# An mLSTM cell and a squared-ReLU feed-forward on one core: gates in two steps, a bf16 mask, the first tiles in another order, and loads placed after y's store

## The chip, the cores and the metric

The kernel runs on one core of one Trainium2 chip. The metric is the device time in microseconds (us); the time before is the median of five runs.

## The reference

Two blocks are joined. The first is an mLSTM cell with batch B = 4, heads H = 8, sequence S = 768 and head size D = 40, all in float32. The second treats the result as 3072 tokens of 320 values.

```python
for t in range(S):
    m_new  = max(f_gate[t] + m, i_gate[t])
    f_stab = exp(f_gate[t] + m - m_new);  i_stab = exp(i_gate[t] - m_new);  m = m_new
    C = f_stab * C + i_stab * outer(v[t], k[t])          # D x D for each head
    n = f_stab * n + i_stab * k[t]
    y[t] = sigmoid(o_gate[t]) * (C @ q[t]) / max(abs(n @ q[t]), 1)
x = y, transposed to (B*S, H*D) = (3072, 320)
out = maximum(x @ w_in, 0)**2 @ w_out                    # w_in 320 x 2048, w_out 2048 x 320
```

## The kernel before

**Tiles.** The sequence is cut into chunks of 128 positions, six for each batch entry (NB = 6), which gives 24 tiles s = 0 to 23 (NT), each with all 8 heads. Two tiles form a group g = 0 to 11 (NG) of 256 tokens for the feed-forward.

**The cell in chunks.** With the gates summed up inside a chunk (A, and b = i - m - A), the decay between two positions of a chunk is exp(A + b). For a tile the kernel turns k and q (`transposes`), multiplies them (`scores`), makes the decays W (`weigh`), multiplies the two into P (`weighted`), and multiplies P by v, with a column of ones that yields the denominators (`attend`). The state C goes from tile to tile. `normalise` applies the denominator and the output gate and gives x; `turn_rows` turns x into xT, the operand of the feed-forward. From tile 6 and 7 on, turned operands come by DMA through scratch in DRAM: `store_num` and `load_num` carry the numerators, `store_rows` and `load_rows` carry x, and 32x32 block transposes on VectorE finish the turn (`normalise_turned`, `turn_squares`, `turn_kq`). `load_squares` reads k and q from a scratch that `pair_up` writes.

**The gates.** `do_gates` runs once, on 32 rows (batch and head) of 768 columns: a scan for m, some elementwise steps, and a scan for A that restarts at each chunk. `turn_gates` turns b and A. For tiles 0 and 1 A is spread over 128 partitions by TensorE (`spread_A`): a matmul of a 128x128 identity by the causal mask `later` (0 or -1e30), 512 columns wide, starts each half, and four matmuls with selector matrices add the heads' rows. From tile 2 on, A goes by DMA to DRAM (`a_rows`) and is read back broadcast (`load_A`), and GpSimd masks it (`mask`).

**Weights.** The weights come as two 32-bit words for each value. A `Rounding` object takes 26 pieces: `fetch` loads a piece (SyncE's queue, four buffers), `words` converts its parts on ScalarE, and `join` combines them on VectorE and GpSimd and fetches the next piece into the freed buffer.

**Order.** Nothing is planned at run time: the order of the program is the order on each engine, and semaphores guard the data. The program has three parts. The prefix is written out by hand and ends with the first feed-forward matmul; `idle(n)` puts n filler matmuls of 512 columns into TensorE's stream there. Then come eight steps u = 0 to 7 in which tiles 2 to 5 are mixed with the first feed-forward products. Then comes a list of parts (which, g, i) with counter n: which = 1 is a quarter of the first product of group g, which = 2 a step of the second. From n = 8 on, r = n % 8 gives the place in a batch of eight parts and b = 7 + 2 * (n // 8) its tile:

| r | part | around it, before the change |
|---|---|---|
| 0, 1 | second product, steps 0 and 1 of group g | r = 0: turn_squares(b-2), sums; after it normalise and store_rows of b-1; r = 1: load_rows(b-1) |
| 2 to 5 | first product of group g+2 | r = 3 and 5: score and attend_turned of the next tiles; r = 3: store_num, load_num of b |
| 5 | (as above) | ahead: normalise_turned(b), store_rows(b); after: store_num(b+1), load_rows(b), load_num(b+1), load(b+5), load_o |
| 6, 7 | second product, steps 2 and 3 of group g | r = 6: load_squares(b+3); r = 7: load_A(b+4) |

**The second product.** It is made from seven half products (`product`, 16 matmuls of 160 columns each; a matmul is two instructions in float32) with sums of operands (`sums`, `sums_of_weights`) on VectorE. The results are added into two y tiles out of a ring of three (`y_sb`). Step 2 issues the store of y1 (L779), step 3 that of y0 (L784), both on SyncE's queue, which also issues all loads. The first of the next group's adds into y0 reuses the buffer of the y1 stored just before.

Of the kernel before, what the change touches and what calls it, by code (L numbers as in the profile page):

```python
# [29 lines left out]
def kernel(  # L30
# [79 lines left out]
    later = gates.tile([P, P], F32)  # L110
# [5 lines left out]
    def make_consts():  # L116
# [6 lines left out]
        make_identity(nc, ident[:])  # L123

# [120 lines left out]
    def do_gates():  # L245
        nc.vector.tensor_tensor_scan(m_sb[:], f_sb[:], i_sb[:], -1e30, op0=ALU.add, op1=ALU.max)
        nc.vector.memset(f_sb[:, 0:1], 0.0)
        nc.vector.tensor_tensor(f_sb[:, 1:], f_sb[:, 1:], m_sb[:, : S - 1], op=ALU.add)
        nc.vector.tensor_tensor(f_sb[:, 1:], f_sb[:, 1:], m_sb[:, 1:], op=ALU.subtract)
        nc.vector.tensor_scalar_max(f_sb[:], f_sb[:], LOG_ZERO)  # L250
        nc.vector.tensor_tensor_scan(
            A_sb[:], keep[:].rearrange("p c t -> p (c t)"), f_sb[:], 0.0, op0=ALU.mult, op1=ALU.add,
        )
        nc.vector.tensor_tensor(i_sb[:], i_sb[:], m_sb[:], op=ALU.subtract)
        nc.vector.tensor_tensor(i_sb[:], i_sb[:], A_sb[:], op=ALU.subtract)

    def turn_gates():
        for src, dst in ((i_sb, b_T), (A_sb, eA_T)):
            tp = ps_o.tile([P, W], F32, name="tp", tag="o_ps")[:, : S // P * BH].rearrange("p (c r) -> p c r", r=BH)
            for c in range(NB):  # L260
                nc.tensor.transpose(tp[:, c, :], src[:, c * P : (c + 1) * P], ident[:BH, :BH])
            nc.scalar.activation(
                dst[:].rearrange("p b c h -> p c b h"), tp.rearrange("p c (b h) -> p c b h", b=B),
                AF.Copy if dst is b_T else AF.Exp,
            )
# [72 lines left out]
    def spread_A(s):  # L338

        b, c = divmod(s, NB)  # L340
        H2 = H // 2
        d = st.setdefault(s, {})
        d["A"] = []
        for i in range(2):
            A = ps_h.tile([P, H2, P], F32, name="A_ps", tag="h_ps")
            nc.tensor.matmul(
                A[:], lhsT=ident[:], rhs=later[:].unsqueeze(1).to_broadcast([P, H2, P]), start=True, stop=False,
            )
            for h in range(H2):
                nc.tensor.matmul(  # L350
                    A[:, h, :], lhsT=sel[:, i * H2 + h, :], rhs=A_sb[:, c * P : (c + 1) * P],
                    start=False, stop=(h == H2 - 1),
                )
            d["A"].append(A)
# [49 lines left out]
    def transposes(s, o=(False, False), apart=0):  # L404
        d = st[s]
        kqT(s)
        for i, n in enumerate(("kT", "qT")):
            if i > 0 and apart:
                idle(apart)
            tp = bank(o[i])  # L410
            for j in range(PR):
                nc.tensor.transpose(
                    tp[:, j, :], d["kq"][:, i, 2 * j : 2 * j + 2, :].rearrange("p h d -> p (h d)"), ident[:],
                )
            (nc.scalar.copy if i == 0 or s in (0, *range(2, 7)) else nc.vector.tensor_copy)(d[n], tp)
# [13 lines left out]
    def weighted(s, spare=False):  # L429
        d = st[s]  # L430
        d["P"] = []
        for i in range(2):
            t = ffn.tile([P, W], F32, name="r_sb", bufs=4) if spare else work.tile([P, W], F32, name="P_sb")
            t = t[:].rearrange("p (j t) -> p j t", j=PR)
            d["P"].append(t)
            heads = slice(i, H, 2) if s < KQ_SQ else slice(PR * i, PR * (i + 1))
            nc.vector.tensor_tensor(t, d["sc"][i], d["W"][:, heads, :], op=ALU.mult)  # L437
# [380 lines left out]
    fetch(2)  # L818
    make_consts()
    load_part(1, 0)  # L820
    load_part(1, 1)
    load_part(0, 2)
    fetch(1)
# [3 lines left out]
    fetch(1)  # L827
    idle(12)
    transposes(0, apart=4)
    idle(4)  # L830
    scores(0)
    idle(3)
    do_gates()
    rounding.words()
    nc.scalar.dma_start(A_d[:, :], A_sb[:])
    spread_A(0)
    rounding.words()
    turn_gates()
    rounding.join()
    weigh(0)  # L840
    transposes(1, (False, True))
    spread_A(1)
    scores(1, (True, True))
    weigh(1)
    first.close()
# [3 lines left out]
    weighted(0)  # L849
    weighted(1, spare=True)  # L850
# [7 lines left out]
    rounding.step()  # L858
    sum_of_h(0)
    normalise(0)  # L860
    mask(2)
    attend(1)
    sum_of_h(1)
    normalise(1)
    load(3)
    load_A(3)
    rounding.step()
    turn_rows(0)
    idle(4)
    transposes(2)  # L870
    idle(4)
# [128 lines left out]
    for n, (which, g, i) in enumerate(parts):  # L1000
# [39 lines left out]
        if r == 0 and g > 1:  # L1040
            do(turn_squares, b - 2)
            sums(g, ALL, (3,))
# [3 lines left out]
        elif r == 5:  # L1046
            do(normalise_turned, b)
            do(store_rows, b)
        elif r == 7 and g < NG - 1:
            sums(g + 1, ALL, (2,))  # L1050
# [91 lines left out]
        elif r == 5:  # L1142
            do(store_num, b + 1)
            do(load_rows, b)
            do(load_num, b + 1)
            do(load, b + 5)
            for t in range(b + 5, min(b + 7, NT)):
                load_o(t)
        elif r == 6:
# [3 lines left out]
        elif r == 7:  # L1153
            do(load_A, b + 4)
        if which == 2 and g == NG - 1 and i == 0:
            sums(g, ALL, (4,))
# [33 lines left out]
```

## Time and profile before

| quantity | value |
|---|---|
| median of the runs | 533.61 us (532.84 to 534.18, five runs) |
| profiled execution | 535.23 us, span 533.4 us, mean granted TensorE clock 0.989 |
| TensorE | busy 513.6 us (96%) |
| TensorE weight load | busy 451.8 us (85%) |
| VectorE | busy 331.7 us (62%) |
| ScalarE | busy 193.9 us (36%) |
| GpSimd | busy 90.6 us (17%) |
| DMA | 68.06 MB, mean 128 GB/s |
| first feed-forward matmul (L649) starts | 32.30 us |

The span runs from the first to the last instruction of one profiled execution; the rest of that execution's time lies around it. In the profile PE is TensorE, PEld its weight load, DVE is VectorE, ACT is ScalarE, POOL is GpSimd, and SP is SyncE; a q behind a name is that engine's queue or sequencer. L649 is line 649 of the kernel before. Rows of the timeline give start, duration, engine, line, operation, output <- input, the number of instructions merged, and in brackets the idle time before it with what ended it. A busy TensorE is not a TensorE at full use: filler counts as busy, and so does a matmul at half clock.

### The profile page before, as it was taken

To read this page: it belongs to the slowest core of one execution; us is meant where nothing else is said; L and a number is where in the kernel's file an instruction comes from. 1 tells how busy PE (TensorE), PEld (TensorE's weight loads), DVE (VectorE), ACT (ScalarE), POOL (GpSimd) and SP (SyncE) were. 2 spreads that over 40 slices of the span, in tenths; PEclk is the share of its full clock that TensorE was granted. 3 is DMA by queue.
4 is the path that set the end of the run, shared out by engine and by line. 5 is a ranking of instruction groups with operands and counts; after the bars stand their busy time and mean duration, and the time that the engine had idled before them with its cause. 6 is when DMAs were issued, how large, how long until landed. Compare 5 with 4: busy or idle time off the path is not lost.

```text
span 533.4 us, 10339 instructions
## 1 busy us (share of the span) xinstructions
PE 513.6 (96%) x3933; PEld 451.8 (85%) x3933; DVE 331.7 (62%) x638; ACT 193.9 (36%) x460; POOL 90.6 (17%) x110
## 2 busy tenths in 40 slices
PE   9998999999999889999999989979999999999997
PEld 4886788886898778898898888878898898998997
DVE  8479977869875744755855845735864864441451
ACT  3776486461735122622333513313714301102100
POOL 3246643221222100100200111110210100000000
PEclk9999899999999989999999999999999999999999
DMA  9999698977677675775775875766764121200000
GB/s 193 218 205 205 145 195 181 213 158 151 149 150 149 162 135 115 163 126 119 165 133 118 173 122 121 166 121 126 156 147 85 55 79 50 63 12 1 26 25 26
DMA packets 239394, 68.06 MB, mean 128 GB/s; under 512 B 185744, under 2 KB 233872, under 8 KB 239344
## 3 DMA queue, kind: packets, MB, share of 16 engines
q1 hardware_dynamic: 239248, 67.20, 60.4%
q8 instruction: 31, 0.51, 0.4%
q10 hardware_dynamic: 96, 0.20, 0.1%
q14 instruction: 19, 0.16, 0.1%
HBM read 55.08 MB, written 17.86 MB: 137 GB/s over the span
## 4 chain that ended last, share of the span: by engine, by line
PE 66%; DMA 13%; SPq 10%; DVE 7%; issue 2%; ACT 1%; POOL 0%; DVEq 0%; POOLq 0%; ACTq 0%
PE h_ps L649 23%; PE h_ps L743 20%; PE h_ps L660 6%; DMA x_rows<-x_sb 4%; PE tp L424 3%; SPq L562 3%; DMA out_dram<-y_sb 3%; DMA num_rows<-tn 3%; PE h_ps L689 2%; SPq L309 2%; SPq L324 2%; PE numT L534 2%; SPq L618 2%; PE hp L460 2%; PE idle L802 2%
## 5 line engine op out<-in xcount | busy, mean ns | idle before, releaser
L649 PE MATMUL h_ps<-xT,w_in 128*128 128x256 f32 x768 | 173.8, 384 | 1.8 <-POOL w_in L215 0.9
L649 PEld LDWEIGHTS h_ps<-xT,w_in 128*128 128x128 f32 x768 | 145.4, 192 | 23.4 <-issue 1.4
L675 ACT ACTIVATE r_sb<-h_ps 128x512 f32<-128x512 f32 x96 | 50.1, 598 | 113.0 <-PE h_ps L660 56.6
L743 PE MATMUL h_ps<-w_out,g 128*128 128x160 f32 x528 | 78.4, 304 | 8.8 <-DVE y_sb L759 8.8
L743 PEld LDWEIGHTS h_ps<-w_out,g 128*128 128x128 f32 x528 | 74.4, 193 | 10.3 <-DVE y_sb L759 10.0
L682 DVE TENSOR_TENSOR g<-r_sb 128x512 f32<-128x512 f32 x96 | 65.5, 732 | 10.0 <-ACT r_sb L675 10.0
L383 ACT ACTIVATE W_sb<-A_bc,b_T 128x128 f32<-128x128 f32 x176 | 53.8, 388 | 21.4 <-POOL A_bc L359 21.3
L437 DVE TENSOR_TENSOR P_sb<-tp,W_sb 128x512 f32<-128x512 f32 x46 | 29.6, 685 | 49.9 <-PE numT L534 32.3
L743 PE MATMUL h_ps<-T,S 128*128 128x160 f32 x352 | 52.3, 302 | 0.0
L743 PEld LDWEIGHTS h_ps<-T,S 128*128 128x128 f32 x352 | 48.8, 190 | 1.6 <-issue 0.9
L660 PE MATMUL h_ps<-xT,w_in 64*128 64x256 f32 x384 | 49.0, 392 | 0.0
L660 PEld LDWEIGHTS h_ps<-xT,w_in 64*128 64x128 f32 x384 | 34.8, 186 | 12.1 <-issue 9.1
L759 DVE TENSOR_TENSOR y_sb<-y_sb,h_ps 128x160 f32<-128x160 f32 x44 | 14.1, 320 | 44.8 <-PE h_ps L743 44.8
L763 ACT COPY y_sb<-h_ps 128x160 f32<-128x160 f32 x11 | 3.2, 292 | 102.0 <-PE h_ps L743 102.0
L359 POOL TENSOR_SCALAR_AFFINE_SELECT A_bc<-A_bc 128x1024 f32<-128x1024 f32 x22 | 27.2, 1236 | 71.8 <-ACT kq L369 62.6
L396 POOL TENSOR_TENSOR vw<-va,W_sb 128x328 f32<-128x328 f32 x20 | 17.8, 891 | 80.1 <-ACT W_sb L383 64.5
L743 PE MATMUL h_ps<-w_out,S 128*128 128x160 f32 x176 | 27.5, 313 | 2.5 <-DVE y_sb L759 2.5
L743 PEld LDWEIGHTS h_ps<-w_out,S 128*128 128x128 f32 x176 | 26.1, 201 | 2.8 <-DVE y_sb L759 2.8
L490 POOL TENSOR_TENSOR Cd<-C,kq 128x164 f32<-128x164 f32 x15 | 6.9, 463 | 120.9 <-DVE C L551 106.7
L759 DVE TENSOR_TENSOR y_sb<-h_ps,y_sb 128x160 f32<-128x160 f32 x11 | 3.6, 324 | 37.5 <-DMA out_dram<-y_sb 24.2
L424 PEld LDWEIGHTS tp<-kqT 40*128 40x128 f32 x384 | 24.8, 188 | 2.4 <-issue 1.1
L369 ACT ACTIVATE kq<-A_bc 64x512 f32<-64x512 f32 x30 | 18.8, 628 | 21.7 <-DMA A_bc<-a_rows 19.8
(119 smaller groups left out, 620.0 us busy)
## 6 DMA issues: line engine op xcount, KB each, us to landing
A_bc<-a_rows SPq DMA_DIRECT2D x23, 512.0 KB, 5.0
raw<-in_moe_w_out_dram SPq DMA_DIRECT2D x16, 320.0 KB, 3.6
num_rows<-tn SPq DMA_DIRECT2D x18, 256.0 KB, 2.7
kq<-num_rows SPq DMA_DIRECT2D x72, 64.0 KB, 2.2
kqT<-kq_rows SPq DMA_DIRECT2D x34, 128.0 KB, 3.1
raw<-in_moe_w_in_dram SPq DMA_DIRECT2D x8, 512.0 KB, 5.1
kq<-in_k_dram SPq DMA_DIRECT2D x24, 160.0 KB, 3.9
va<-in_v_dram SPq DMA_DIRECT2D x24, 160.0 KB, 4.7
```

Source lines behind the costliest of these rows:

```text
L359: nc.gpsimd.affine_select(A[:], A[:], compare_op=ALU.is_ge, fill=-1e30, base=0, pattern=[[0, H], [1, P]], channel_multiplier=-1,)
L369: nc.scalar.activation(e[rows], st[s]["A"][0][rows, PR * i : PR * (i + 1), :], AF.Exp)
L383: nc.scalar.activation(d["W"][:, i * n + h, :], A[i][:, h, :], AF.Exp, bias=b_T[:, b, c, i * n + h : i * n + h + 1],)
L396: nc.gpsimd.tensor_tensor(d["vw"][:], d["va"][:], d["W"][:, :, P - 1 : P].to_broadcast([P, H, D1]), op=ALU.mult,)
L424: nc.tensor.matmul(sc[i][:, j, :], lhsT=d["kT"][rows, j, :], rhs=d["qT"][rows, j, :], start=True, stop=True,)
L437: nc.vector.tensor_tensor(t, d["sc"][i], d["W"][:, heads, :], op=ALU.mult)
L649: nc.tensor.matmul(hs[i][:, n, :], lhsT=w_in[:, a, fb * P : (fb + 1) * P], rhs=xT[:, :, a, :], start=(n == 0 and a == 0), stop=False,)
L660: nc.tensor.matmul(hs[i][:, n, :], lhsT=w_in2[rows, 2 * pp + n, :], rhs=xT[rows, :, 2, :], start=False, stop=(n == 1),)
L675: nc.scalar.activation(rs[-1][:], h[:], AF.Relu)
L682: nc.vector.tensor_tensor(g4[:, :, i, :], r[:], r[:], op=ALU.mult)
L743: nc.tensor.matmul(to, lhsT=lhsT[:, p], rhs=rhs[:, p, :], start=(start and p == 0), stop=(p == NPAIR - 1), skip_group_check=True,)
L759: add = lambda to, a, b: nc.vector.tensor_tensor(to, a, b, op=ALU.add)
```

## The change

- `later` becomes bf16, and a bf16 identity `identb` is made beside it; the mask's matmul uses both. The mask is put into PSUM by a function of its own, `spread_mask`, and `spread_A` handles one half of a tile.
- `do_gates` is split into `do_A` and `do_b` with a range of chunks. Chunks 0 and 1 are done first, with their turn; chunks 2 to 5 follow while tile 0 is worked on.
- `transposes` is split by k and q; the copies all go to ScalarE. The P tiles of tile 1 use the two xT buffers.
- In the prefix loads, fetches, joins and filler are placed anew: `idle` goes from 12, 4, 4, 3, 4, 4 to 11 and 2.
- In the list of parts, `turn_squares(b - 2)` moves from r = 0 to r = 1; `load(b + 5)` and its `load_o` move from the end of r = 5 to r = 6, behind the y1 store that step 2 issues. For tile 9 normalise, store and load of x move from r = 5 to n = 14 and n = 15.

```diff
-    later = gates.tile([P, P], F32)
+    later = gates.tile([P, P], BF16)
+    identb = gates.tile([P, P], BF16)
...
+        make_identity(nc, identb[:])
...
+    def do_A(c0, c1):
+        t0, t1 = c0 * P, c1 * P
+        now = slice(t0, t1)
         nc.vector.tensor_tensor_scan(
-            A_sb[:], keep[:].rearrange("p c t -> p (c t)"), f_sb[:], 0.0, op0=ALU.mult, op1=ALU.add,
+            m_sb[:, now], f_sb[:, now], i_sb[:, now], m_sb[:, t0 - 1 : t0] if c0 else -1e30, op0=ALU.add, op1=ALU.max,
         )
+        if c0 == 0:
+            nc.vector.memset(f_sb[:, 0:1], 0.0)
+            t0 = 1
+        f, m = f_sb[:, t0:t1], m_sb[:, t0:t1]
+        nc.vector.tensor_tensor(f, f, m_sb[:, t0 - 1 : t1 - 1], op=ALU.add)
+        nc.vector.tensor_tensor(f, f, m, op=ALU.subtract)
+        nc.vector.tensor_scalar_max(f_sb[:, now], f_sb[:, now], LOG_ZERO)
+        nc.vector.tensor_tensor_scan(
+            A_sb[:, now], keep[:, c0:c1].rearrange("p c t -> p (c t)"), f_sb[:, now], 0.0, op0=ALU.mult, op1=ALU.add,
+        )
+
+    def do_b(c0, c1):
+        now = slice(c0 * P, c1 * P)
+        nc.vector.tensor_tensor(i_sb[:, now], i_sb[:, now], m_sb[:, now], op=ALU.subtract)
+        nc.vector.tensor_tensor(i_sb[:, now], i_sb[:, now], A_sb[:, now], op=ALU.subtract)
...
+    def spread_mask(s, i):
+        A = ps_h.tile([P, H // 2, P], F32, name="A_ps", tag="h_ps")
+        nc.tensor.matmul(
+            A[:], lhsT=identb[:], rhs=later[:].unsqueeze(1).to_broadcast([P, H // 2, P]), start=True, stop=False,
+        )
+        st.setdefault(s, {}).setdefault("A", []).append(A)
+
+    def spread_A(s, i):
+        b, c = divmod(s, NB)
+        A = st[s]["A"][i]
+        for h in range(H // 2):
             nc.tensor.matmul(
...
+                A[:, h, :], lhsT=sel[:, i * (H // 2) + h, :], rhs=A_sb[:, c * P : (c + 1) * P],
+                start=False, stop=(h == H // 2 - 1),
+            )
...
-            (nc.scalar.copy if i == 0 or s in (0, *range(2, 7)) else nc.vector.tensor_copy)(d[n], tp)
+        nc.scalar.copy(d[("kT", "qT")[i]], tp)
...
-            t = ffn.tile([P, W], F32, name="r_sb", bufs=4) if spare else work.tile([P, W], F32, name="P_sb")
+            if spare:
+                t = xts.tile([P, GT, 3, P], F32, name="xT")[:].rearrange("p g c t -> p (g c t)")[:, :W]
+            else:
+                t = work.tile([P, W], F32, name="P_sb")[:]
...
     load_part(0, 1)
-    fetch(2)
     make_consts()
+    fetch(1)
+    load_part(0, 2)
     load_part(1, 0)
     load_part(1, 1)
-    load_part(0, 2)
-    fetch(1)
     load_o(0)
     load_o(1)
     load_part(1, 2)
-    fetch(1)
-    idle(12)
-    transposes(0, apart=4)
-    idle(4)
+    fetch(3)
+    idle(11)
+    spread_mask(0, 0)
+    spread_mask(0, 1)
+    transpose(0, 0)
+    do_A(0, 2)
+    do_b(0, 2)
+    spread_A(0, 0)
+    turn_gates(0, 2)
+    transpose(0, 1)
+    spread_A(0, 1)
     scores(0)
-    idle(3)
-    do_gates()
+    weigh(0)
+    do_A(2, NB)
     rounding.words()
+    transpose(1, 0)
+    transpose(1, 1, o=True)
+    weighted(0)
+    do_b(2, NB)
     nc.scalar.dma_start(A_d[:, :], A_sb[:])
-    spread_A(0)
-    rounding.words()
-    turn_gates()
-    rounding.join()
-    weigh(0)
-    transposes(1, (False, True))
-    spread_A(1)
+    for i in range(2):
+        spread_mask(1, i)
+        spread_A(1, i)
+    turn_gates(2, NB)
     scores(1, (True, True))
     weigh(1)
+    rounding.join()
     first.close()
...
-    weighted(0)
-    weighted(1, spare=True)
     load(2)
...
     attend(0)
-    rounding.step()
+    weighted(1, spare=True)
+    rounding.words()
     sum_of_h(0)
     normalise(0)
+    rounding.join()
     mask(2)
     attend(1)
     sum_of_h(1)
+    turn_rows(0)
+    idle(2)
     normalise(1)
     load(3)
     load_A(3)
-    rounding.step()
-    turn_rows(0)
-    idle(4)
+    rounding.words()
     transposes(2)
-    idle(4)
+    rounding.join()
     sigmoid(2)
...
         if r == 0 and g > 1:
+            sums(g, ALL, (3,))
+        elif r == 1 and g > 1:
             do(turn_squares, b - 2)
-            sums(g, ALL, (3,))
...
-        elif r == 5:
+        elif r == 5 and b > 9:
             do(normalise_turned, b)
             do(store_rows, b)
...
         elif r == 5:
             do(store_num, b + 1)
-            do(load_rows, b)
+            if b > 9:
+                do(load_rows, b)
             do(load_num, b + 1)
+        elif r == 6:
+            if n == 14:
+                normalise_turned(9)
+                store_rows(9)
             do(load, b + 5)
             for t in range(b + 5, min(b + 7, NT)):
                 load_o(t)
-        elif r == 6:
             do(load_squares, b + 3)
             if n == 14:
                 turn_squares(8)
         elif r == 7:
             do(load_A, b + 4)
+            if n == 15:
+                load_rows(9)
```

## The prediction

> **What bounds the kernel now.** I read the page first, then the list of waits, then the timeline wherever TensorE idles, and the windows for its clock.
>
> The page's first section gives busy time and share of the span:
>
> ```profile
> PE 513.6 (96%) x3933; PEld 451.8 (85%) x3933; DVE 331.7 (62%) x638; ACT 193.9 (36%) x460; POOL 90.6 (17%) x110
> ```
>
> TensorE (PE) is busy 96%, but its prefix contains filler (`idle`) and f32 mask matmuls. Time can only come from PE instructions that disappear, idle stretches, or halved clock. The list of waits (total us, times, longest) names the idling in the main loop:
>
> ```profile
> DVE y_sb L759 <- DMA out_dram<-y_sb: 24.2, 5, 5.7
> ...
> PE h_ps L743 <- DVE y_sb L759: 11.3, 6, 3.2
> ```
>
> PE waits six times for VectorE's (DVE's) add into y, five of them because that add rewrites a buffer whose store hasn't landed. The timeline of one such place (start, duration, instruction, [idle before <- releaser]):
>
> ```profile
> 350.16 2.98 SPq L562 DMA_DIRECT2D kq<-num_rows  x4
> ...
> 353.24 0.39 SPq L296 DMA_DIRECT2D kq<-in_k_dram  x1
> ...
> 353.73 0.53 SPq L296 DMA_DIRECT2D va<-in_v_dram  x1
> ...
> 354.31 1.60 SPq L324 DMA_DIRECT2D og<-in_o_gate_dram  x2
> ...
> 356.01 1.38 SPq L779 DMA_DIRECT2D out_dram<-y_sb  x1
> ...
> 359.71 0.33 DVE L759 TENSOR_TENSOR y_sb<-h_ps,y_sb 128x160 f32<-128x160 f32 x1 [4.46 <-DMA out_dram<-y_sb]
> ...
> 360.09 2.44 PE L743 MATMUL h_ps<-w_out,g 128*128 128x160 f32 x16 [3.25 <-DVE y_sb L759]
> ```
>
> y's data were ready at 348.5 (add at 348.19 plus 0.32), but SyncE's queue (SP) reached the store at 356.01, after k, v and two output gates. It landed 3.6 us later. The six PE gaps are 2.52 (184.03), 2.52 (197.19), 0.79, 0.52, 1.74 and 3.25: 11.34 us. The first is another kind: DVE stands at L574 for tile 9's numerators, with the adds queued behind it:
>
> ```profile
> 179.27 0.17 DVE L574 TENSOR_SCALAR dm<-kq 128x8 f32<-128x8 f32 x1 [3.69 <-DMA kq<-num_rows]
> ...
> 184.03 4.12 PE L743 MATMUL h_ps<-w_out,S 128*128 128x160 f32 x16 [2.52 <-DVE y_sb L759]
> ```
>
> Both early gaps are followed by a lower PE clock (windows; the third number from the right is the clock):
>
> ```profile
> 184.00:186.00 2.00, 1.97 (x8) 1.97 (x9) 2.00 (x4) 0.00 (x0) 0.97 (x2) 0.56 0.81 262
> 186.00:188.00 2.00, 2.00 (x11) 2.00 (x10) 1.44 (x2) 0.00 (x0) 0.36 (x1) 0.58 0.34 56
> ```
>
> That costs 2 x (0.44 + 0.42) = 1.72 us; 198 to 202, at 0.50 and 0.67, costs 1.66. From 374 on the windows show no PE gap.
>
> The prefix ends when the first feed-forward matmul starts, held by xT of tile 1:
>
> ```profile
> 32.30 3.72 PE L649 MATMUL h_ps<-xT,w_in 128*128 128x256 f32 x16 [0.62 <-ACT xT L634]
> ```
>
> **What the Trainium skill says.** "TensorE: Matmul & The Clock Gate", section "What's actually happening": after an idle window of about 3.4 us the clock is halved, and the window runs free of the kernel. The trace agrees in size (two drops to one half after 2.52 us gaps), and the free phase fits that the 3.25 us gap shows clock 1.00 after it. "DMA: Bandwidth & Descriptors", section "Queues, rings and completion order": each engine takes descriptors in ring order, so a store issued after loads also waits behind their packets. Here y's store landed in 3.1 to 4.0 us behind the loads, and in 2.2 us at 392.15, where there were none.
>
> **The change, part by part.** The sum is against the profiled execution, 535.23 us (span 533.4 and 1.8 around it). It lies 1.62 above the median of 533.61, which I subtract at the end.
>
> *Main loop, loads behind the store.* In iterations 13, 21, 29, 37 and 45 (tiles b = 9 to 17 have a tile b+5) k, v and two output-gate loads move from r = 5 to r = 6, so y1's store passes 4 DMAs. Their SP time, L296 to L779, is 3.15, 2.97, 2.76, 3.11 and 2.77 us. The landing falls from 3.1-4.0 to about 2.2, so the store lands some 4 us sooner. The add came 2.5, 2.2, 3.4 and 4.95 us after its product's end (at 237.55, 277.25, 318.18 and 359.71): the first three vanish, the last leaves 0.8. So 0.79 + 0.52 + 1.74 + 3.25 = 6.3 us goes, and about 0.5 returns. The loads come one store issue (0.4 to 0.6 us) later; their tiles are five ahead, so the work on four tiles covers it; without it the wait would be that issue. The squares' loads (L309, 4 DMAs) already stood behind that store and keep their place.
>
> *Main loop, tile 9.* normalise and store_rows of tile 9 leave r = 5 for the end of n = 14, its load_rows (4 DMAs) goes to the end of n = 15. DVE then doesn't stand at 179; the 2.52 gap and its 1.72 of clock go. The second gap (2.52 + 1.66) goes by the earlier store. But x of tile 9 is now late. The adds of step 2 end near 181.8; normalise takes 2.1 (2.3 in other places); the store is issued near 184.1, lands 5 us later; SP meanwhile issues k, v, gates (3.0), squares (2.7), y0 (0.5), A (0.4) and reaches load_rows near 191.1; four issues of 0.47 and 1.8 to landing give 195, and the transpose (0.57) 195.6. PE without the gaps wants this xT at 192.8: a new wait of 2.8 us, with 0.2 for S2 queued behind normalise. Bounds 0 and 6; I take 3.0, plus half a clock drop, 0.85.
>
> *Main loop, turn_squares from r = 0 to r = 1.* DVE does it after y's add, the squares and normalise. It releases the sums, but now stands right before its consumer. In the undisturbed batch at 400:
>
> ```profile
> 400.24 0.20 DVE L583 COPY x_sb<-x_sb 128x64 f32<-128x64 f32 x1
> ...
> 401.29 7.07 PE L649 MATMUL h_ps<-xT,w_in 128*128 128x256 f32 x32
> ```
>
> DVE is free at 400.44, 0.57 later is 401.01: 0.28 us to spare. I cost it at nothing; without that cover each of 8 batches (g = 2 to 9) would add what is lacking. Behind it waits only step 1's last add (needed two products later).
>
> Main loop: -11.34 - 3.38 + 3.0 + 0.85 + 0.5 = **-10.4 us**.
>
> *Prefix.* Filler falls from 12+4+4+3+4+4 to 11+2: the chain has 12 in 5.30 and the later fours in 0.87 each, so about 4.4 us of PE work goes. The four f32 masks take 0.86 + 1.05 + 0.86 + 1.05 = 3.82 in the chain; I price a bf16 one like a filler matmul of the same 512 columns, 0.22 warm and 0.44 cold: about 1.3 for four. The bf16 identity adds a memset and a select on POOL (0.20 + 0.29), done by 4.4, before the first mask near 5.7. The gates for two chunks take a third of the rows 1.75, 0.94, 0.95, 0.55, 1.75: about 2.2 us from their landing at 3.99, so A is there at 6.2 instead of 10.07; the other four chunks follow on DVE to about 11. Stepping through the engines with the durations shown: A spread by 9.9, scores of tile 0 by 11.0, its weights (2 x 1.14 + 2 x 0.2 on ACT) by 12.3 (before 18.4); W of tile 1 by 18.6 (22.2); x of tile 0 at 21.7 (27.4); join 1 until 23.6, x of tile 1 at 27.2 (31.2), xT at 28.3 (32.3). The split adds some 7 short DVE instructions of 0.06 fixed time, inside this. q's copy for tile 1 goes from DVE (0.69) to ACT (0.58). Filler removed near 25 to 28 leaves PE idle about 2.5 us: half a drop, 0.85. SP issues the same bytes; its order puts v 0 and k, q 1 before the raw weights, but the gates og 2 and 3, which ACT needs before xT, landed at 28.4 before and may again: xT then is near 29.9. I take 29.0, a shift of 3.3. I don't subtract the half drop, since the stage to 61 us is set by DVE (its chain 41.80 to 60.66 has no idle), whose work is unchanged and moves along. ACT's extra pair of words (1.3) after W of tile 2 lies in its 3.14 us wait at 43.6. Tile 1's P in xT's buffers: turn_rows comes after its readers on PE anyway. Prefix: **-3.3 us**, bounds -0.5 and -5.
>
> Sum -13.7: 521.5 for the profiled execution, 519.9 against the median; I say 520.
>
> **Rivals.**
> *The wait moves to x's round trip.* The gap after tile 9 is 6 us with a whole drop (1.7), the batch at 356 keeps 2, the prefix gives 1: 535.2 - 14.7 + 7.7 + 2 - 1 = 529.2, or 527.6 against the median. For: the chain that ended last runs through x_rows and L618 for most of 164 to 350. Against: xT landed 5 us before use in the batch at 356.
> *The store isn't set by the loads* but by SP's earlier waits (L618, L562), and only the prefix counts: 530. Against: L779 follows L324 directly in all five.
> *Slower: turn_squares becomes the wait of every batch.* Place: DVE at r = 1, PE at L649. If xT or DVE is late by 2.5 us, each with a 1.7 us drop, 8 x 4.2 = 34 is added to 533.6 - 18: about 550. It decides from 13.7/8 = 1.7 us of wait per batch. For: only 0.28 us to spare. Against: DVE has no wait there once y's store has landed, and the profile has xT there at 353.5 for 359.
> *The prefix hands its time back*: og's landing and a clock drop leave 0; 523.
>
> **How the numbers follow.** Forecast 0.66 (own range 515 to 525), prefix handed back 0.08, round trip 0.13, store not set by loads 0.06, slower 0.05, nothing 0.02. All gaps and drops gone with a 5 us prefix would be 513.9 by the median. The range 513.5 to 529 leaves out the slower cases and half the weak gains. 0.2% (1.1 us) is about what a measurement can tell: faster 0.92, same 0.03, slower 0.05.
>
> **What would show it.** After: L649's first start near 29; A's scan of 256 columns near 5.6; masks of about 0.4 us or less; L779 ahead of L296 in the five batches and no "DMA out_dram" wait of DVE over 1 us; one gap of 2 to 4 us before L649 near 185 to 192 released by L625. Wrong if L743 still waits for y_sb, if L625 releases L649 in most batches, or if L649 starts after 31.

## The result and the profile after

| | before | after |
|---|---|---|
| median of the runs beside each other | 533.65 us (47 runs) | 540.37 us (28 runs) |
| ratio of the comparisons | | 1.0096, 95% interval 1.0076 to 1.0117 |
| profiled execution | 535.23 us, span 533.4 | 542.76 us, span 541.0 |
| mean granted TensorE clock there | 0.989 | 0.958 |
| first feed-forward matmul | 32.30 us (L649) | 38.30 us (L667) |

The change makes the kernel slower by about 1%, not faster by 2.6%. This ratio and those below leave out the slowest executions of a kernel (here 9 of 28, the profiled one of after among them), so it is smaller than that of the two medians, and the trace's absolute times show the mechanism near its largest.

Lines have moved: L649 is now L667, L743 is L761, L759 is L777, L625 is L643, L562 is L580, L613 is L631, L618 is L636, L779 is L797. The first section of the page after:

```profile
PE 518.8 (96%) x3911; PEld 459.3 (85%) x3911; DVE 333.0 (62%) x644; ACT 195.3 (36%) x463; POOL 89.8 (17%) x112
```

There are 22 matmuls fewer, and yet PE is busy 5.2 us longer: matmuls last longer, so the clock is to be looked at. The page's second section prints it by slice (13.5 us each, tenths of full speed):

```profile
PEclk9559989999999996999999999999999999999999
```

Slices 2 and 3 are near one half (before they were at 9), and one slice, at 203 to 216 us, is at 6. In this trace these two places carry the loss. The list of waits shows the second from another side (total us, times, longest):

```profile
PE h_ps L667 <- DVE xT L643: 9.9, 2, 9.7
...
DVE y_sb L777 <- DMA out_dram<-y_sb: 6.6, 2, 3.6
...
PE h_ps L761 <- DVE y_sb L777: 1.5, 1, 1.5
```

The wait for y, 11.3 us before, is down to 1.5. VectorE still waits twice for a store, which the prediction had ruled out, but only 1.5 us of waiting for y reaches PE. In its place stands one wait of 9.7 us for xT. **The place of the old 3.25 us gap** in the timeline (start, duration, instruction, [idle before <- releaser]):

```profile
360.65 1.84 SPq L580 DMA_DIRECT2D kq<-num_rows  x4
...
362.59 0.38 SPq L797 DMA_DIRECT2D out_dram<-y_sb  x1
...
363.06 0.40 SPq L310 DMA_DIRECT2D kq<-in_k_dram  x1
...
364.65 4.51 PE L761 MATMUL h_ps<-w_out,g 128*128 128x160 f32 x32
364.91 0.33 DVE L777 TENSOR_TENSOR y_sb<-h_ps,y_sb 128x160 f32<-128x160 f32 x1 [2.87 <-PE h_ps L761]
```

The store stands ahead of k, v and the gates; the add that rewrites y now waits for its product (L761), not for the store, and PE runs without a gap. **Tile 9**, the same view:

```profile
189.91 0.17 DVE L592 TENSOR_SCALAR dm<-kq 128x8 f32<-128x8 f32 x1
...
191.51 0.20 DVE L601 COPY x_sb<-x_sb 128x64 f32<-128x64 f32 x1
...
192.58 1.74 SPq L580 DMA_DIRECT2D kq<-num_rows  x4
...
194.42 0.38 SPq L797 DMA_DIRECT2D out_dram<-y_sb  x1
194.89 0.38 SPq L631 DMA_DIRECT2D x_rows<-x_sb  x1
...
198.28 4.58 SPq L323 DMA_DIRECT2D kqT<-kq_rows  x4
...
202.95 0.51 SPq L802 DMA_DIRECT2D out_dram<-y_sb  x1
203.57 0.38 SPq L348 DMA_DIRECT2D A_bc<-a_rows  x1
203.99 3.31 SPq L636 DMA_DIRECT2D xT<-x_rows  x4
...
210.11 0.58 DVE L643 STREAM_TRANSPOSE xT<-xT 128x384 f32<-128x384 f32 x1 [10.08 <-DMA xT<-x_rows]
...
210.74 1.65 PE L667 MATMUL h_ps<-xT,w_in 128*128 128x256 f32 x3 [9.69 <-DVE xT L643]
```

x of tile 9 is in SBUF at 191.7, but SP issues its store at 194.89 and the load back at 203.99. PE, ready at 201.05, stands until 210.74. The windows add the clock (third number from the right):

```profile
206.00:208.00 2.00, 0.00 (x0) 0.00 (x0) 0.00 (x0) 0.00 (x0) 0.00 (x0) 0.50 0.90 200
...
214.00:216.00 2.00, 2.00 (x7) 1.62 (x6) 0.99 (x1) 0.00 (x0) 0.00 (x0) 0.54 0.51 131
```

So the wait also costs some 5 us of busy PE at half clock (210.74 to 216), 2.5 us more. **The prefix**: matmuls of the same kind take twice as long, and hardly any idle stands between them:

```profile
6.88 1.15 PE L364 MATMUL A_ps<-A_sb,sel 32*128 32x128 f32 x8 [0.92 <-DVE A_sb L261]
...
13.20 2.07 PE L364 MATMUL A_ps<-A_sb,sel 32*128 32x128 f32 x8
...
17.61 0.58 PE L275 MATMUL tp<-ident,i_sb 32*128 32x32 f32 x4
...
38.30 5.40 PE L667 MATMUL h_ps<-xT,w_in 128*128 128x256 f32 x16 [1.28 <-ACT xT L652]
```

```profile
10.00:12.00 2.00, 2.00 (x21) 1.88 (x22) 1.93 (x4) 2.00 (x9) 0.33 (x1) 0.76 1.46 168
...
18.00:20.00 2.00, 2.00 (x17) 1.93 (x18) 0.00 (x0) 1.62 (x8) 0.00 (x0) 0.50 1.02 338
...
42.00:44.00 2.00, 2.00 (x12) 1.49 (x13) 1.23 (x3) 2.00 (x5) 0.74 (x1) 1.00 0.00 0
```

From 12 to 40 us the clock is one half, although PE is busy in 2.00 of 2.00 us in twelve of these fourteen windows; here it comes back 3.5 us after the wide L667 matmuls begin. In this pair of traces the first feed-forward matmul is 6.0 us later, the part around 185 us 8.1 later, and the end 7.6: the prefix lost about 8, and the list of parts, which was to bring 10, brought about 0.5.

### The profile page after: what moved, and what is told of

Same layout as the page of the kernel before. It is cut to its first block, busy times and chain, and to the rows that moved or that the text cites. A ratio compares the mean times of both kernels' runs of the same rounds, so it can differ in the third digit from the quotient of the medians.

```text
span 541.0 us, 10300 instructions
## 1 busy us (share of the span) xinstructions
PE 518.8 (96%) x3911; PEld 459.3 (85%) x3911; DVE 333.0 (62%) x644; ACT 195.3 (36%) x463; POOL 89.8 (17%) x112
## 4 chain that ended last, share of the span: by engine, by line
PE 74%; DVE 9%; DMA 9%; SPq 5%; issue 2%; ACT 0%; DVEq 0%; ACTq 0%
PE h_ps L761 26%; PE h_ps L667 25%; PE h_ps L678 6%; PE tp L439 3%; DMA x_rows<-x_sb 3%; PE h_ps L707 2%; PE numT L552 2%; PE hp L478 2%; SPq L323 2%; DVE g L700 2%; DMA kq<-num_rows 1%; DMA num_rows<-tn 1%; DVE mag L212 1%; PE tp L423 1%; SPq L636 1%
## 5 line engine op out<-in xcount | busy, mean ns | idle before, releaser
L667 PE MATMUL h_ps<-xT,w_in 128*128 128x256 f32 x768 | 178.2, 391 | 12.4 <-DVE xT L643 9.9
L667 PEld LDWEIGHTS h_ps<-xT,w_in 128*128 128x128 f32 x768 | 148.1, 196 | 36.1 <-DVE xT L643 10.7
L761 PE MATMUL h_ps<-w_out,g 128*128 128x160 f32 x528 | 75.5, 300 | 0.0
L700 DVE TENSOR_TENSOR g<-r_sb 128x512 f32<-128x512 f32 x96 | 67.3, 751 | 10.0 <-ACT r_sb L693 10.0
L761 PEld LDWEIGHTS h_ps<-w_out,g 128*128 128x128 f32 x528 | 72.9, 190 | 0.3 <-issue 0.2
L455 DVE TENSOR_TENSOR P_sb<-tp,W_sb 128x512 f32<-128x512 f32 x46 | 29.7, 684 | 51.3 <-PE numT L552 30.7
L761 PE MATMUL h_ps<-T,S 128*128 128x160 f32 x352 | 52.4, 302 | 0.3 <-DVE S L756 0.3
L761 PEld LDWEIGHTS h_ps<-T,S 128*128 128x128 f32 x352 | 48.7, 190 | 2.1 <-issue 1.2
L777 DVE TENSOR_TENSOR y_sb<-y_sb,h_ps 128x160 f32<-128x160 f32 x44 | 14.0, 318 | 38.9 <-PE h_ps L761 38.7
L330 DVE STREAM_TRANSPOSE kqT<-kqT 128x1024 f32<-128x1024 f32 x17 | 21.0, 1238 | 13.1 <-DMA kqT<-kq_rows 13.0
L439 PEld LDWEIGHTS tp<-kqT 40*128 40x128 f32 x384 | 26.0, 194 | 2.5 <-issue 1.1
L439 PE MATMUL tp<-kqT 40*128 40x128 f32 x384 | 27.7, 282 | 0.1
L761 PE MATMUL h_ps<-w_out,S 128*128 128x160 f32 x176 | 25.8, 300 | 1.5 <-DVE y_sb L777 1.5
L761 PEld LDWEIGHTS h_ps<-w_out,S 128*128 128x128 f32 x176 | 24.5, 190 | 1.8 <-DVE y_sb L777 1.8
```

Of the source, the lines that this page charges most:

```text
L330: nc.vector.transpose(t, t)
L439: nc.tensor.matmul(sc[i][:, j, :], lhsT=d["kT"][rows, j, :], rhs=d["qT"][rows, j, :], start=True, stop=True,)
L667: nc.tensor.matmul(hs[i][:, n, :], lhsT=w_in[:, a, fb * P : (fb + 1) * P], rhs=xT[:, :, a, :], start=(n == 0 and a == 0), stop=False,)
L700: nc.vector.tensor_tensor(g4[:, :, i, :], r[:], r[:], op=ALU.mult)
L761: nc.tensor.matmul(to, lhsT=lhsT[:, p], rhs=rhs[:, p, :], start=(start and p == 0), stop=(p == NPAIR - 1), skip_group_check=True,)
L777: add = lambda to, a, b: nc.vector.tensor_tensor(to, a, b, op=ALU.add)
```

## The experiments

**Theory 1**: the prefix is slower because the clock falls once filler and wide f32 masks are gone; either (1a) the 0.92 us gap ahead of the spread of A starts it, or (1b) it is the stretch of narrow matmuls. **Theory 2**: the y gaps are closed, and tile 9's late x takes the gain back. **Rivals**: `turn_squares` at r = 1 delays the batches; the new order of the prefix is longer in itself; the bf16 mask matters. Each kernel was timed beside the kernel before; ratios are to it, with 95% intervals. The runs are from several chips, so kernels are compared by these ratios and not by their times.

| run | kernel | ratio |
|---|---|---|
| e1_prefix | before + the new prefix | 1.0061 (1.0031 to 1.0092) |
| e2_loop | before + the new list of parts | 1.0048 (1.0027 to 1.0068) |
| e3_fill | after + filler in the gap before A | 1.0104 (1.0070 to 1.0138) |
| e4_tile9 | after, tile 9 as before | 0.9978 (0.9954 to 1.0002) |
| e5_f32mask | after, mask and identity in f32 | 1.0120 (1.0083 to 1.0157) |
| e6_warm | after + much filler | 1.0050 (1.0030 to 1.0070) |
| e7_store | before + only the loads behind y's store | 0.9870 (0.9832 to 0.9909) |
| e8_rows | before + new list, tile 9's load ahead of the squares | 0.9928 (0.9901 to 0.9955) |
| e9_slack | after + filler where PE has slack | 1.0017 (0.9985 to 1.0048) |
| e10_best | e8 and tile 9's store ahead of tile 10's numerators | 0.9912 (0.9882 to 0.9943) |
| e11_turn | e7 + `turn_squares` at r = 1 | 0.9884 (0.9844 to 0.9923) |
| e12_both | e9 with tile 9 as before | 0.9894 (0.9855 to 0.9932) |

**Which half is slower?** e1 takes the new prefix with the old list, e2 the old prefix with the new list:

```
e1 (on before):                          e2 (on before):
-  later = gates.tile([P, P], F32)       -  do(turn_squares, b - 2)        (r == 0)
+  later = gates.tile([P, P], BF16)      +  elif r == 1 and g > 1:
+  identb = gates.tile([P, P], BF16)     +      do(turn_squares, b - 2)
...                                      ...
+  do_A(0, 2)                            -  elif r == 5:
+  do_b(0, 2)                            +  elif r == 5 and b > 9:
...                                      ...
+  idle(2)                               +  if n == 15:
...                                      +      load_rows(9)
```

> The kernel before, with the new prefix alone (gates in two steps, bf16 mask, new order and less filler); the list of parts is as before. Theory 1, the prefix lost its clock: the first feed-forward matmul starts near 38 us with the TensorE clock at one half from about 11 to 41 us, and the time is 6 to 8 us above the kernel before (ratio 1.011 to 1.015). Theory 2, the prefix is as good as forecast and the loss is all in the list of parts: the start is near 29 us and the ratio is 0.994.

> The kernel before, with the new list of parts alone (loads behind y1's store, turn_squares at r = 1, tile 9's x late); the prefix is as before. Theory 1: y's gaps go (11.3 us and 3.4 us of clock), the wait for tile 9's xT comes (about 9.7 us and 2 us of clock, small gaps 2 us): ratio 0.996 to 1.001. Theory 2, the list of parts carries the whole loss: ratio 1.015 or more.

Both are slower, and 0.61% and 0.48% make up the 0.96% of the whole. Neither is at the number expected: e1 lies between its two theories, and e2 a little above the 0.996 to 1.001 of the first. A window and the first feed-forward matmul of e1:

```profile
18.00:20.00 2.00, 2.00 (x12) 2.00 (x11) 1.14 (x3) 1.99 (x4) 1.42 (x2) 0.50 1.04 318
```

```profile
34.09 3.69 PE L667 MATMUL h_ps<-xT,w_in 128*128 128x256 f32 x16 [1.28 <-ACT xT L652]
```

Half clock, here from 16 to 33, and a start 1.8 us later than the 32.30 before. There is no PE gap before A in this execution (L364 at 6.60 follows L423 directly), so 1a isn't needed: the clock fell without that gap. e2 has the wait of 9.6 us:

```profile
201.08 9.61 PE L649 MATMUL h_ps<-xT,w_in 128*128 128x256 f32 x32 [9.62 <-DVE xT L625]
...
358.69 6.53 PE L649 MATMUL h_ps<-xT,w_in 128*128 128x256 f32 x29 [0.96 <-DVE xT L625]
```

Among 8 batches only one waits long: `turn_squares` isn't the wait of every batch.

**What pulls the clock down in the prefix?** e3 fills the gap, e5 gives the mask its f32 back:

```
e3:      transpose(0, 0)                e5: -    later = gates.tile([P, P], BF16)
     +   idle(4)                            +    later = gates.tile([P, P], F32)
                                            -    identb = gates.tile([P, P], BF16)
                                            +    identb = ident
```

> The changed kernel with four filler matmuls of 512 columns put after k's transposes of tile 0, where TensorE stood idle for 0.92 us before A was there. Theory 1a, that one gap and the missing wide matmuls took the clock down: the clock stays at 1.00 through the prefix, the first feed-forward matmul starts near 29 to 30 us instead of 38, and the time is 8 us or more under the changed kernel (ratio to the kernel before about 0.994). Theory 1b, the whole stretch of narrow matmuls takes the clock down whatever happens at 6 us: the clock still falls between 10 and 15 us and the time is as that of the changed kernel (ratio 1.01). Theory 2, the order of the work holds the start and not the clock: the start stays at 38 us with the clock up.

> The changed kernel with the causal mask and its identity in f32 again: four wide f32 matmuls (two instructions each) instead of four bf16 ones. If the wide f32 masks were what kept the clock up in the kernel before, the clock stays at 1.00 or falls clearly later than at 11 to 18 us, the first feed-forward matmul starts before 32 us in spite of some 2.5 us more mask work, and the time is 2 us or more below the changed kernel. If the masks don't matter for the clock, it falls as in the changed kernel and the time is 1 to 3 us above it (masks at half clock, 4 x 0.9 us more).

In e3 the clock falls at 17.55 us, although PE has no gap ahead of A, and the kernel is no faster: 1a falls. (The prefix without this filler lost the clock at 11.04 us in after, at 15.92 in e1 and at 15.19 in e4, so the later time by itself says little.) In e5 it falls at 20.08 us, after the last f32 mask (15.29 to 16.42): the masks did not hold it for good. They also take time themselves, and the intervals of e5 and after overlap. The mask's dtype alone isn't what loses the clock. e6 and e9 then hold the clock by filler only:

```
e6: idle(4) after transpose(0, 0); each mask of tile 1 written four times over; idle(4) before
    turn_gates(2, NB); idle(4) for idle(2); idle(8) after transposes(2)
e9: idle(2) after transpose(0, 0); idle(6) after turn_gates(2, NB);
    idle(4) for idle(2); idle(8) after transposes(2)
```

> The changed kernel with wide bf16 filler through its prefix: four after k's transposes of tile 0, each mask of tile 1 written four times, four ahead of the second turn of the gates, four instead of two after xT of tile 0, eight after the transposes of tile 2. Theory 1, the clock: it stays at 1.00 to 32 us, the first feed-forward matmul starts near 29 to 30 us, and the time is 4 us or more below the changed kernel. Rival, the order of the work: the clock is up and the start is still at 32 us or later.

> The changed kernel with filler only where TensorE waits for other engines: two after k's transposes of tile 0, six after the second turn of the gates, four instead of two after xT of tile 0, eight after the transposes of tile 2; the masks are written once. If filler ahead of the second turn (16 wide matmuls in the run with much filler, which put the turn 3 us late) is what kept the clock up, the clock falls again between 11 and 18 us, and the first feed-forward matmul starts at 32 us or later. If little filler in slack is enough, the clock stays up, the second turn is near 15 us instead of 17.9, the start is near 29 us, and the time is 3 us below the run with much filler (ratio to the kernel before about 0.999 with the late x still in it).

In both profiled executions the clock does not fall in the prefix. In e6 the start is 32.00, as its rival had it: filler on the path cost what the clock gave. In e9 the filler lies where PE would wait for ACT or DVE. The start in e6, then a window and two starts in e9:

```profile
32.00 3.69 PE L669 MATMUL h_ps<-xT,w_in 128*128 128x256 f32 x16 [0.66 <-ACT xT L654]
```

```profile
18.00:20.00 2.00, 2.00 (x21) 2.00 (x19) 1.43 (x3) 1.99 (x4) 1.39 (x2) 1.00 1.14 296
```

```profile
28.97 3.69 PE L667 MATMUL h_ps<-xT,w_in 128*128 128x256 f32 x16 [0.66 <-ACT xT L652]
...
198.31 6.97 PE L667 MATMUL h_ps<-xT,w_in 128*128 128x256 f32 x22 [9.71 <-DVE xT L643]
```

The start at 28.97 shows that the new order is not longer in itself; the rival falls. But the runs of e9 spread: three with a mean granted clock of 0.99 took 527.1 to 529.0 us, seven with 0.981 to 0.987 took 530.2 to 532.5, and four with 0.961 to 0.965 took 538.3 to 542.4. So the same program kept the clock in some executions and lost it in others. That those at 0.961 to 0.965 lost it in the prefix was not seen: the one trace is of an execution at 0.99. With the more plentiful filler of e6, 21 of 22 runs lie at 0.984 to 0.987.

**What does the clock follow?** This was read from the traces afterwards; no run was made to test it. In all 14 traces each stretch at one clock lasts a whole number of 3.41 us, apart from the last, which the end cuts off. In after the clock is at half from 11.04 to 41.76 us, nine such periods, in e1 from 15.92 to 32.99, five. So the clock is set period by period. PE's busy time doesn't tell what the next period gets, but this sum does: for every matmul instruction in a period take its columns, twice in f32 (256 columns in f32 take 0.23 us, 512 in bf16 take 0.22), and multiply by its contraction rows over 128. A bound of 3,070 on this sum, fitted to the 2,143 periods of these traces, puts all but 3 right: above it the next period has full clock, below it half. Columns without the rows leave 19 wrong, and the best bound on busy time 45, where only 76 periods are followed by half clock.

| trace | period (us) | PE busy | sum | clock in it | clock in the next |
|---|---|---|---|---|---|
| after | 7.63 to 11.04 | 3.41 | 3,150 | 1.00 | 0.50 |
| e1 | 12.51 to 15.92 | 3.29 | 2,300 | 1.00 | 0.50 |
| e9 | 14.56 to 17.97 | 3.25 | 4,720 | 1.00 | 1.00 |
| after | 21.28 to 24.69 | 3.41 | 1,910 | 0.50 | 0.50 |
| before | 23.82 to 27.24 | 3.41 | 3,820 | 1.00 | 1.00 |
| after | 38.35 to 41.76 | 3.41 | 3,990 | 0.50 | 1.00 |

The first row is one of the three exceptions. The fourth and fifth hold the same kind of work, products of 82 and 41 columns: at full clock it passes the bound, at half clock PE gets through half as much of it and stays below. So one weak period is enough, and the clock stays away until filler, 128-row transposes or wide products come. Where the periods begin differs between executions (the first recorded change of the clock is at 4.21 us in after, 5.68 in e1 and 4.95 in e4, which have one prefix), and the half clock lasted nine, five and five periods there.

**What does tile 9 cost?** e4 is after with tile 9 as it was; e8 and e10 keep its new place but let SP reach its DMAs sooner:

```
e4: -  elif r == 5 and b > 9:        e8:    elif r == 6:                 e10: as e8, and
    +  elif r == 5:                         ...                               +  if n != 13:
    -  if b > 9:                            +   if n == 14:                          do(load_num, b + 1)
    +  do(load_rows, b)                     +       load_rows(9)                 elif r == 6: ...
    (n == 14 and n == 15 calls out)             do(load_squares, b + 3)          store_rows(9)
                                            (n == 15 call out)                +  load_num(10)
```

> The changed kernel with tile 9 treated as every other tile (normalise and store of x ahead at r = 5, load_rows at r = 5); the loads stay behind y1's store. Theory: the wait of 9.7 us for xT and the half clock after it (2 us) go, the stall of VectorE before step 3 (2.5 us and 1.7 us of clock) comes back: 6 to 8 us under the changed kernel (about 533, ratio to the kernel before 0.995 to 1.000). Rival, the late xT is SyncE's queue being late anyway: the wait of L667 for the transposed x stays above 5 us and the time moves by less than 2 us.

> The kernel before with the new list of parts, in which tile 9's load_rows is issued at n = 14 ahead of load_squares instead of at the end of n = 15. It passes four loads of squares (4.6 us of SyncE's time in the changed kernel), y0's store and A's load. If the late x is a matter of SyncE's order, the wait of L649 for tile 9's xT falls from 9.6 us to 2 us or less, the half clock after it goes, and the ratio is 0.98 to 0.99. If the round trip through DRAM is what takes long, the wait stays above 6 us.

> The kernel before with the new list of parts, but tile 9's x issued earlier on SyncE's queue: load_num of tile 10 follows tile 9's store of x instead of preceding y1's store, and tile 9's load_rows goes ahead of the squares' loads at n = 14. If the late xT is SyncE's order and the landing of x behind other transfers, the store of x is issued near 183.7 instead of 186.4, the load near 188.5 instead of 191, and the wait of 2.9 us and the half clock after it go: ratio 0.975 to 0.985. If the round trip is bound otherwise, the wait stays near 3 us and the ratio is 0.993.

e4 against after's 1.0096: tile 9's move alone costs 1.2%, over 6 us, although without it a wait for y of 2.5 us is back, as a row of e4's waits shows:

```profile
PE h_ps L761 <- DVE y_sb L777: 4.6, 4, 2.5
```

e8 against e2: the load ahead of the squares brings 1.2% again. Its chain, from the timeline:

```profile
186.38 0.38 SPq L613 DMA_DIRECT2D x_rows<-x_sb  x1
...
190.95 2.15 SPq L618 DMA_DIRECT2D xT<-x_rows  x4
...
193.14 2.75 SPq L309 DMA_DIRECT2D kqT<-kq_rows  x4
...
194.80 0.58 DVE L625 STREAM_TRANSPOSE xT<-xT 128x384 f32<-128x384 f32 x1 [3.26 <-DMA xT<-x_rows]
...
195.44 8.86 PE L649 MATMUL h_ps<-xT,w_in 128*128 128x256 f32 x32 [2.87 <-DVE xT L625]
```

The wait is 2.9 us instead of 9.6, not the 2 or less expected. In e10 x's store goes out at 183.94, yet its load only at 190.30, since k, v and the gates lie between them (v's issue alone took 2.04): the wait stays at 2.78 us, and e10 misses what was expected of it.

**What are the moved loads and `turn_squares` worth?** e7 makes one edit to before, e11 two:

```
         elif r == 5:                                    (e7 and e11)
             do(store_num, b + 1)
             do(load_rows, b)
             do(load_num, b + 1)
+        elif r == 6:
             do(load, b + 5)
             for t in range(b + 5, min(b + 7, NT)):
                 load_o(t)
-        elif r == 6:
             do(load_squares, b + 3)
e11 as well: do(turn_squares, b - 2) from r == 0 to r == 1
```

> The kernel before with one move alone: k, v and output-gate loads of tile b+5 from r = 5 to r = 6, behind y1's store. By the prediction's step the four later gaps (6.3 us) and most of the second early one go, the first stays, as tile 9's normalise is where it was: 6 to 8 us less, ratio 0.985 to 0.989. If SyncE's earlier waits hold the store (the rival that only the prefix counts), the gaps stay and the ratio is 0.997 to 1.000.

> The kernel before with loads behind y1's store and turn_squares at r = 1 (with the sums ahead), tile 9 as before: against the run with the loads alone (ratio 0.987) it shows what turn_squares' new place does. By the prediction's step it costs nothing: 0.987. By the waits of L667 for DVE's transpose in the changed kernel without tile 9's move (0.19, 0.64 and 1.39 us) it costs about 2 us: 0.991.

e7 is the best single edit: -1.3%, 6.9 us, as expected, although the first gap, which was to stay, is down from 2.52 to 1.1 us in its trace; no run shows why. Two rows of e7's list of waits, and the same two of e11's:

```profile
PE h_ps L743 <- DVE y_sb L759: 3.8, 6, 1.1
...
PE h_ps L649 <- DVE xT L625: 0.3, 1, 0.3
```

```profile
PE h_ps L649 <- DVE xT L625: 2.2, 2, 1.4
...
PE h_ps L743 <- DVE y_sb L759: 1.4, 3, 0.7
```

`turn_squares` at r = 1 takes 2.4 us out of the wait for y and puts 1.9 into the wait for xT; the ratios, 0.9870 and 0.9884, don't differ. It moves a wait and is worth nothing that these runs can tell.

**Both causes undone.** e12 puts the diffs of e9 and e4 together. (Its expectation has `turn_squares` at r = 0; the edit leaves it at r = 1.)

> After's kernel with both suspected causes undone: tile 9's x goes round as before (turn_squares at r=0, normalise and store of x(9) at its own parts r=4/r=5), and the prefix has filler in its slack (idle(2) after transpose(0,0), idle(6) after turn_gates(2,NB), idle(4) for idle(2), idle(8) after transposes(2)). Nothing is left out. If the two causes are all there is (the clock in the prefix, tile 9's x round trip), this adds up: the list with tile 9 as before gave 0.998 with its first ffn matmul at 34.6 us; the filler brought that matmul to 29.0, so 5.6 us of 530 less: 0.987, about 523 us, first ffn matmul near 29, waits of the main matmul for xT under 2 us, clock at full speed up to there. If the filler holds the clock only in some runs (the spread of 527 to 542 in the run with filler alone), the median is 0.99 to 0.998 with a spread of 10 us or more. If the trace of the filler run was a lucky one and the prefix costs what it cost without filler, 0.998.

The first feed-forward matmul of the profiled execution and a window; below them the first feed-forward matmul of e11:

```profile
29.95 3.69 PE L667 MATMUL h_ps<-xT,w_in 128*128 128x256 f32 x16 [0.66 <-ACT xT L652]
```

```profile
48.00:50.00 2.00, 2.00 (x9) 1.05 (x8) 1.93 (x4) 0.60 (x2) 1.38 (x1) 0.50 1.08 307
```

```profile
31.13 3.72 PE L649 MATMUL h_ps<-xT,w_in 128*128 128x256 f32 x16 [0.57 <-ACT xT L634]
```

The clock holds through the prefix and falls only later, at half from 47.71 to 54.54 us; before has such a drop too, at 61.37. 0.9894 is 0.8% below e4, as far as e9 lies below after: where the filler holds the clock, the two causes add up. Six of its nine runs, at a clock of 0.99, took 520.5 to 526.2 us, and the ratio is theirs; three at 0.974 took 533.5 to 537.3. But it isn't better than e7, which leaves the prefix as it was and whose six runs lie between 520.8 and 526.7. Nor is it better than e11 (0.9884), which has the same list of parts and the old prefix: in the traces the new prefix starts the feed-forward 1.2 us sooner (29.95 against 31.13), and in the time no gain can be told, where 3.3 us were forecast. Of the kernels tried, e7 is the one to take: 1.3% under before, where after is 1% over it.

## Why the prediction was wrong

- **Loads behind the store (right in mechanism, size cut).** L797 precedes L310, and the waits for y went from 11.3 us to 1.5 in after. Alone (e7) 3.8 us of waits for y stayed, and the gain was 6.9 us (4.8 to 8.9 by the interval of the ratio) where I had 10.0 (6.3 and 2.52, with 1.66 of clock, less 0.5). The landing of 2.2 us held in later batches (2.1 for the store at 309.08 in e7) but not in tile 9's: with the loads issued behind it, it took 3.7 there (issued at 188.87, add released at 192.55).
- **Tile 9's x (the step that failed, in size).** "A new wait of 2.8 us ... I take 3.0, plus half a clock drop, 0.85", with bounds 0 and 6. Measured: 9.7 us and about 2.5 of clock, outside the bounds. Taking off the 8.1 us by which all is later there, the sum comes apart into three terms. x was normalised when I said (191.71 less 8.1 is 183.6; I had 184.1), but SP was standing at L580 for tile 10's numerators and then issued their loads, so the store left 2.7 us later than I said. SP then reached the load after 9.1 us instead of 7.0, as the squares took 4.58 us instead of 2.7. And the load landed 6.1 us after its issue instead of 3.7, one of its issues taking up to 1.52 us; the load of A_bc stood directly ahead of it. These make 2.7 + 2.1 + 2.4 = 7.2, with the 2.8 of the forecast 10.0; PE came 0.2 us later than I had it, which leaves 9.8 of the measured 9.7. I had counted the DMAs that the load is moved past, but not the wait of SP that the *store* is moved behind.
- **turn_squares at no cost (right as a sum).** It moved a wait (e11). The rival of a slower kernel had the right line, L649 released by L625, but the wrong extent: one batch, and through the load of x, not through the new place of `turn_squares`: e11 has the new place without the late load, and its longest such wait is 1.4 us.
- **Prefix (the other step that failed).** "A shift of 3.3 ... I don't subtract the half drop." The steps through the engines were right: I had the scores of tile 0 by 11.0 and they ended at 11.0; its weights by 12.3, measured 11.6; the start at 29.0, and e9 at full clock gave 28.97. What failed was the clock: I asked only about one 2.5 us idle stretch near 25 us. It fell at 11.04 us and stayed at half to 41.76, with PE busy for 29.4 of these 30.7 us. That is a start at 38.30, 9.3 us after the forecast, in the profiled execution, and 0.6% in the ratio of e1. I read filler as PE work that goes; it was also what held the clock (e6, e9). And even with the clock held (e12 against e11) the 3.3 us don't show in the time; why is open.
- **The rivals.** Two of them named the two places that failed, tile 9's round trip (6 us with a drop) and the prefix handing its time back (to nothing), each as a smaller gain; neither had a loss, and together they were not priced.
- **The Trainium skill**, "TensorE: Matmul & The Clock Gate", section "What's actually happening", ties the clock to how busy PE has been in a window of about 3.4 us. Read with the profile's busy column this misled: 2.00 of 2.00 us busy with narrow or short matmuls (128x41, 32 rows by 128, 40 rows by 128) went with a clock of 0.50. The window itself agrees with the traces, in its 3.41 us and in a phase that differs between executions. The prediction's gaps of 2.52 us are shorter than that, so no period needed to be idle throughout: PE was busy for 0.9 us of the one from 180.83 to 184.25, which the first drop followed. That the phase is the reason for the spread of e9 and e12 fits, but no run here shows it.

The sum with measured terms: e1's +0.6% and e2's +0.5%, against -0.6% and -1.9% forecast. That filler in the prefix holds the clock in the profiled executions of e6 and e9 is shown. The sum of columns and rows is a fit to traces that were there already: a run with filler placed by it, in several executions with a trace each, is what would test it.

## What to carry to other kernels

Filler or wide matmuls in a stretch of narrow ones are not spare PE time: before you remove them, ask what else in the next microseconds would hold the clock, and price the whole stretch at half speed, up to the next work that is wide and uses all 128 rows. When a store and a load of one round trip are moved, follow the issuing queue over both: what it waits for ahead of the store counts as much as what it issues ahead of the load. Test a package edit by edit: here one three-line move was worth 1.3%, and the rest of the package more than gave it back.

## What the runs showed of the hardware

- A PE that the profile shows as busy all the time can stay at half clock: 24 us in after (12 to 36 us), 16 us in e1 (16 to 32). In after the clock came back 3.5 us after L667 began (38.30 to 41.76); in e1, e3, e4 and e5 it came back 1.1 to 2.4 us before it (at 32.99, 31.20, 32.26 and 33.73), during f32 transposes of 128 rows that follow two filler matmuls, or just after them.
- The clock changed only at whole multiples of 3.41 us from its last change, in all 14 traces, and the clock of such a period went with the columns times rows that PE had worked off in the period before it (bound near 3,070; 3 of 2,143 periods against it). Up to its first record, at 4 to 7 us, the profile prints a clock of 1.00, but a filler matmul takes 0.43 us there and 0.22 later.
- The same program had the clock in one execution and not in another: e12's runs lie some 10 us apart at 0.99 and 0.974.
- The idle wait of 9.69 us in after came with half clock from 205.60 to 215.84, some 5 us of it with PE busy. Waits of 2.87 us (e8), 2.78 (e10) and twice 2.52 (before) were each followed by one period of 3.41 us at half clock, and the one of 3.25 us in before by none.
